# Splitting every attention step of heads 3 to 32, with a product moved to GpSimd and TensorE's order left to the scheduler

## The chip, the cores and the metric

The kernel runs on one core of a Trainium2 chip. The metric is device time in microseconds (us) of one execution, from launch to end. Five engines work side by side, each through its own queue in order: TensorE (PE; PEld is its weight load), VectorE (DVE), ScalarE (ACT), GpSimd (POOL) and SyncE (SP), which issues the DMAs. An instruction that waits for a semaphore holds up everything behind it on its engine.

## The reference

Three layers in a row, all in float32:

```
# 1: attention with pooled queries, B=4, H=8 (32 heads), S=1152, D=64, T=576 pooled queries
q_pool = q.reshape(B, H, S // 2, 2, D).mean(axis=3)
scores = scale * q_pool @ k.T;  attn = softmax(scores);  x = attn @ v
# 2: four experts of causal attention over T=576, each token weighted by the top 2 of a gate
logits = x @ w_gate
for e in range(4): out += weight_e * (softmax(causal(q_e k_e.T)) @ v_e @ wo[e])
# 3: channel mixing, with the token before mixed in (mu)
k = relu(xk @ w_k);  v = k * k @ w_v;  out = sigmoid(xr @ w_r) * v
```

## The kernel before

Layer 1 goes through 32 heads (index 0 to 31; the title counts from 1). A head is nine steps. Step `si` of `s1_job` takes two tiles of 128 keys against 288 queries each: `qk` (L778, L779) multiplies into a PSUM tile `st` (two of them rotate), `ew` takes the exponential on ScalarE (L786) into `p`, and `pv` multiplies `p` by the values, four steps later (`LAG`), into an accumulator `bank` (four PSUM banks rotate among all users).

High precision comes from splitting: a float32 number is written as a rounded high part (fp32r) and the rest, and products of the parts are summed. For `pv` there are two forms, chosen for each step by the tables `S0` and `S1`. A step marked `'sv'` is split: ScalarE copies `p` to its high part `ph` (L64), VectorE subtracts to get `pl` (L71), and `pv` is three fp32r matmuls (L813, L814, L815). A step marked `'n'` is not split: `pv` is one float32 matmul (L806), which the profile shows as two records. Before, steps 0, 3 and 6 of every head from the third on are `'n'`.

Beside these steps run tasks, put at places between steps by tables of start and end: the load of a later head's q, k and v; its preparation `s1_prep` (transposes, splits into `sk`, then `dup_q` and `dup_k`, 14 DMAs per head that copy the parts to `QA`, `QB`, `KA`, `KB` and the small block `BD`); and `s1_max`, which finds each query's largest score (L735 and L750 on TensorE, L737 and L751 on VectorE). Its end, `max_finish`, transposes the maxima (L402), copies them to `mr` (L403, VectorE) and sends them by DMA to a row of `QB` (L410, L411). `L779` of the next head reads that row, so a head can't complete its first step before the row has landed. `normaliser` fetches each head's row sums by DMA (`sd`), inverts them, and brings them back spread over partitions (`R`); L835 multiplies by it into `XT`, on VectorE. From the ninth head on, the work of layer 2 for the batch before stands between the steps, and the splitting of layer 3's weights (`w3st`) runs on VectorE and ScalarE.

Order: a scheduler orders each engine's instructions by its own estimate of when they can start, except that from three steps ahead of head 2 to the end of the heads TensorE keeps the order in which the program is written (L1095, `manual_schedule`).

Of the kernel before, what the change touches and what calls it, by code (L numbers as in the profile page):

```python
# [55 lines left out]
def tile_kernel(ctx: ExitStack, tc: tile.TileContext, q, k, v, w_gate, wq, wk, wv, wo,  # L56
                mu_k, mu_r, w_k, w_v, w_r, out):
    nc = tc.nc
    LAG, LO, HB = G["LAG"], G["LO"], G["HB"]
# [14 lines left out]
    T = S // 2  # L74
# [9 lines left out]
    HT = T // 2  # L84
# [39 lines left out]
    def f32(ap):  # L124
        return ap.bitcast(F32)
# [12 lines left out]
    def act_hi(dst, src):  # L138
        nc.scalar.activation(dst, src, AF.Copy)
# [14 lines left out]
    def later(n, fn):  # L154
        pending.append((now[0] + n, fn))
# [13 lines left out]
    def drive(steps, tasks, drain=False, first=0):  # L169
        def fill(t):  # L170
            for x in tasks:
                x.run(t)

        for i, st in enumerate(steps, first):
            now[0] += 1
            if st.qk:
                st.qk()
            if st.ew:
                st.ew()
            lagged.append(st)  # L180
            if len(lagged) > LO and lagged[-1 - LO].ew2:
                lagged[-1 - LO].ew2()
                lagged[-1 - LO].ew2 = None
            pv = lagged.pop(0).pv if len(lagged) > LAG else ()
            m = len(pv) + 1
            for j in range(m):
                fill(i + (j + 1) / m - 1e-6)
                if j < len(pv):
                    pv[j]()
            run_later()  # L190
        if drain:
            for st in lagged:
# [353 lines left out]
    def s2_out(b):  # L546
        def make(dt):
# [12 lines left out]
            def ew():  # L560
# [36 lines left out]
    BD = [s1.tile([P, P], F32R, name=f"BD{i}") for i in range(2)]  # L597
# [29 lines left out]
    def s1_prep(hh):  # L627
        first = hh < G["nf1"]
        kr, qr = raw.pop(hh)
        i = hh % NK  # L630
        own = (slice(0, D), slice(D, P))
        KAi, KBi, QAi, QBi = KA[i], KB[i], QA[i], QB[i]
        qp = s1a.tile([QW, NQ * D], F32, tag="qp", name=f"qp{hh}")
        sk = None if first else s1a.tile([P, 2, SW + HT], F32R, tag="sk", name=f"sk{hh}")
# [44 lines left out]
        qhalf = (slice(0, HT), slice(HT, T))  # L679
# [201 lines left out]
    CW = G["CW"]  # L881
# [68 lines left out]
    steps, tasks = [], []  # L950
# [61 lines left out]
    for hh in range(NH):  # L1012
        z = "0" if hh < H else "1"
        if hh + 1 < NH:
# [311 lines left out]
```

## Time and profile before

| | us |
|---|---|
| median of 3 runs (lowest, highest) | 1110.75 (1109.9, 1113.37) |
| the profiled execution's own time | 1113.59 |
| its span, first to last instruction | 1111.9 |
| TensorE busy, share of the span | 1030.4, 93% |
| VectorE busy, share | 788.0, 71% |
| ScalarE busy, share | 582.7, 52% |
| GpSimd busy, share | 183.5, 17% |
| mean granted TensorE clock | 0.970 |

The shares are averages over unlike stages: the heads take about the first 760 us, the last batch's layer 2 and layer 3 the rest, in which VectorE and ScalarE do much less. TensorE's records overlap (a matmul's record starts while the one before still drains), so its busy time is more than its work; the distance from one start to the next tells what a matmul costs.

### The profile page before, as it was taken

What the parts mean: (1) busy time and instruction counts of PE and PEld (TensorE: products, weight loads), DVE (VectorE), ACT (ScalarE), POOL (GpSimd) and SP (SyncE); (2) the same over time, 40 slices, a digit from 0 to 9 for tenths busy, and PEclk for the clock granted to TensorE, in tenths of its full rate; (3) what the DMA queues carried; (4) which work ended last, traced back from release to release, by engine and by line L of the source; (5) the groups of instructions that cost most, each with busy time, mean ns of one, the idle gap of its engine ahead of it and who ended that gap; (6) DMA issues with size and microseconds to landing.
All of it is one profiled execution on the core that took longest, in us unless ns stands there. A gap on an engine that the chain in (4) does not pass through costs nothing.

```text
span 1111.9 us, 18276 instructions
## 1 busy us (share of the span) xinstructions
PE 1030.4 (93%) x6450; PEld 892.8 (80%) x6450; DVE 788.0 (71%) x1647; ACT 582.7 (52%) x999; POOL 183.5 (17%) x279
## 2 busy tenths in 40 slices
PE   6898999999988899998989999989898799999998
PEld 4687888987777797787779888878776688888887
DVE  5787887888779679888878777786867534444442
ACT  5456777566556456666656566664455212222222
POOL 6223111110212000120110011021012001111110
PEclk9899999999999999999999999999998899999999
DMA  4556666646544664565456544337345321111100
GB/s 112 140 130 150 132 152 146 158 117 156 133 121 104 156 156 123 146 163 136 108 122 180 126 114 108 86 100 221 122 138 163 110 81 39 38 38 39 39 19 19
DMA packets 144397, 129.08 MB, mean 116 GB/s; under 512 B 71401, under 2 KB 106658, under 8 KB 144306
## 3 DMA queue, kind: packets, MB, share of 16 engines
q1 hardware_dynamic: 144306, 127.92, 44.9%
q8 instruction: 51, 0.84, 0.3%
q14 instruction: 40, 0.33, 0.1%
HBM read 63.24 MB, written 20.07 MB: 75 GB/s over the span
## 4 chain that ended last, share of the span: by engine, by line
PE 56%; DVE 16%; DMA 15%; SPq 4%; ACT 4%; issue 3%; POOL 2%; DVEq 0%; ACTq 0%; POOLq 0%
PE stw L1159 9%; PE sth L1123 7%; PE str L1146 4%; PE bank L806 4%; PE stq L348 4%; PE st L778 3%; PE st L779 3%; PE bank L735 3%; DVE PM L737 3%; DMA R<-scr 3%; DVE pl L71 3%; PE bank L504 3%; PE bank L813 2%; PE bank L814 2%; PE stv L281 2%
## 5 line engine op out<-in xcount | busy, mean ns | idle before, releaser
L786 ACT ACTIVATE p<-st 128x576 f32<-128x576 f32 x288 | 186.1, 647 | 130.6 <-PE st L779 123.5
L737 DVE TENSOR_REDUCE PM<-bank 128x1 f32<-128x384 f32 (+1 forms) x390 | 208.3, 547 | 48.7 <-PE bank L735 46.5
L778 PE MATMUL st<-QA,KA 128*128 128x288 f32 x576 | 186.1, 336 | 2.5 <-ACT p L786 2.0
L779 PE MATMUL st<-QB,KB 65*128 65x288 f32 x576 | 167.3, 304 | 0.3 <-DMA QB<-mr 0.3
L735 PE MATMUL bank<-KA,QA 128*128 128x384 f32 (+1 forms) x390 | 154.8, 408 | 11.7 <-DVE KB L145 3.6
L71 DVE TENSOR_TENSOR pl<-p,ph 128x576 fp32r<-128x576 f32 x190 | 147.1, 775 | 21.8 <-ACT ph L64 19.9
L64 ACT ACTIVATE ph<-p 128x576 fp32r<-128x576 f32 x190 | 129.6, 683 | 19.3 <-PE bank L814 12.6
L778 PEld LDWEIGHTS st<-QA,KA 128*128 128x128 f32 x576 | 113.2, 197 | 14.0 <-ACT p L786 3.2
L806 PE MATMUL bank<-p,VF 128*65 128x288 f32 x384 | 118.6, 406 | 0.2
L779 PEld LDWEIGHTS st<-QB,KB 65*128 65x128 f32 x576 | 113.5, 197 | 3.9 <-DMA QB<-mr 0.7
L813 PE MATMUL bank<-ph,VV 128*65 128x288 f32 x384 | 115.4, 300 | 1.3 <-DVE sk L145 1.0
L815 PE MATMUL bank<-pl,VV 128*65 128x288 f32 x384 | 114.2, 298 | 0.0
L814 PE MATMUL bank<-ph,VV 128*64 128x288 f32 x384 | 114.1, 297 | 0.0
L735 PEld LDWEIGHTS bank<-KA,QA 128*128 128x128 f32 (+1 forms) x390 | 77.2, 200 | 28.8 <-DVE PM L737 5.3
L71 POOL TENSOR_TENSOR VV<-VF,VV 128x576 fp32r<-128x576 f32 x32 | 43.0, 1345 | 307.7 <-ACT VV L64 292.3
L1123 PE MATMUL sth<-xkh,wk 128*128 128x256 f32 x512 | 91.4, 279 | 1.2 <-ACT relu L1130 1.2
L1130 ACT ACTIVATE relu<-sth 128x512 f32<-128x512 f32 x32 | 17.5, 596 | 122.9 <-PE sth L1123 122.1
L1123 PEld LDWEIGHTS sth<-xkh,wk 128*128 128x128 f32 x512 | 78.7, 188 | 1.8 <-ACT relu L1130 1.4
L1123 PE MATMUL sth<-xkl,wk 128*128 128x256 f32 x256 | 71.4, 279 | 0.0
L504 PE MATMUL bank<-p,V 128*65 128x288 f32 (+5 forms) x288 | 63.1, 351 | 6.0 <-DVE PM L737 4.6
L806 PEld LDWEIGHTS bank<-p,VF 128*65 128x65 f32 x384 | 51.4, 137 | 15.2 <-DVE PM L417 0.9
L490 POOL TENSOR_SCALAR_AFFINE_SELECT p<-p 128x128 f32<-128x128 f32 (+1 forms) x96 | 32.6, 370 | 176.0 <-ACT p L482 172.1
(212 smaller groups left out, 2262.6 us busy)
## 6 DMA issues: line engine op xcount, KB each, us to landing
KA<-sk SPq DMA_DIRECT2D x60, 160.0 KB
qr<-in_q_dram SPq DMA_DIRECT2D x32, 288.0 KB
kr<-in_k_dram SPq DMA_DIRECT2D x32, 288.0 KB
VF<-in_v_dram SPq DMA_DIRECT2D x32, 288.0 KB
QA<-sk SPq DMA_DIRECT2D x120, 72.0 KB
KA<-sk SPq DMA_DIRECT2D x60, 128.0 KB
R<-scr SPq DMA_DIRECT2D x48, 144.0 KB
w3h<-w3st SPq DMA_DIRECT2D x20, 256.0 KB
```

What stands on the lines that cost most here:

```text
L64: nc.scalar.activation(dst, src, AF.Copy)
L71: eng[e].tensor_tensor(dst, src, hi.bitcast(F32), op=ALU.subtract)
L735: nc.tensor.matmul(ps[:n, : 3 * P], QA[i][:, t0 : t0 + n], KA[i][:, 3 * g * P : 3 * (g + 1) * P], start=True, stop=True)
L737: nc.vector.tensor_reduce(pm[:n, c, g : g + 1], ps[:n, : 3 * P], axis=AX.X, op=ALU.max)
L778: nc.tensor.matmul(st[:, n, :HT], KA[i][:, ks], QA[i][:, cs], start=True, stop=False)
L779: nc.tensor.matmul(st[:, n, :HT], KB[i][0 : D + 1, ks], QB[i][0 : D + 1, cs], start=False, stop=True)
L786: nc.scalar.activation(pt, st[:, :, :HT], AF.Exp, scale=1.0 / 16.0)
L806: nc.tensor.matmul(a[: D + 1, :HT], VF[hh % NF][:, c], cell["p"][:, n], start=c == 0, stop=c == NC - 1)
L813: nc.tensor.matmul(a[: D + 1, :HT], vh, ph[:, n], start=c == 0, stop=False)
L814: nc.tensor.matmul(a[:D, :HT], vl, ph[:, n], start=False, stop=False)
L815: nc.tensor.matmul(a[: D + 1, :HT], vh, pl[:, n], start=False, stop=c == NC - 1)
L1123: nc.tensor.matmul(st[:, f // 2, f % 2 * GT : (f % 2 + 1) * GT], w[kt][:, fs], x[:, kt], start=i == 0, stop=i == 3 * KT - 1)
```

## The change

In the table of constants, the keys that change (an entry's place is a step's number where it is a list; positions are in steps relative to a head's first):

| key | before | after | what it sets |
|---|---|---|---|
| `S0`, `S1` | `'n'` at 0, 3, 6, else `'sv'` | `'sv'` at all nine | form of `pv`, heads 3 to 32 |
| `HB` | 3 | 4 | buffers of `ph` and of `pl` |
| `PB` | 6 | 5 | buffers of `p` |
| `xt`, `xt0` | `'v'` | `'g'` | engine of the normalising product: VectorE, GpSimd |
| `mx0`, `mx1` | (-4.5, 4.5) | (-4.2, 4.0) | start and end of `s1_max` |
| `nm` | 1 | 2 | steps from the maxima to their transpose |
| `dup` | 2 | 1 | steps from the split of `sk` to its DMAs |

The rest of the diff:

```diff
@@ max_finish
             nc.tensor.transpose(ps[:5, :P], f32(nm), ident)
-            nc.vector.tensor_copy(mr, ps[:5, :P])
+            act_hi(mr, ps[:5, :P])
@@ s1_prep
-            later(G["dup"], dup_q)
-            later(G["dup"], dup_k)
+            later(G["dup"], dup)
...
-        def dup_q():
+        def dup():
+            n = T % P
+            for up in range(2):
+                nc.sync.dma_start(f32(BD[hh % 2][own[up], up * D : up * D + n]), f32(sk[own[1], 0, SW + HT - n :]))
             for up in range(2):
                 a, z, cs = own[up], own[1 - up], qhalf[up]
                 nc.sync.dma_start(f32(QAi[a, cs]), f32(sk[a, 0, SW:]))
                 nc.sync.dma_start(f32(QAi[z, cs]), f32(sk[a, 1, SW:]))
-                nc.sync.dma_start(f32(QBi[0:D, cs]), f32(sk[a, 0, SW:]))
-            n = T % P
+            dup_k()
             for up in range(2):
-                nc.sync.dma_start(f32(BD[hh % 2][own[up], up * D : up * D + n]), f32(sk[own[1], 0, SW + HT - n :]))
+                nc.sync.dma_start(f32(QBi[0:D, qhalf[up]]), f32(sk[own[up], 0, SW:]))
@@ the end of the heads
-    with tc.manual_schedule(engines={mybir.EngineType.PE}):
-        drive(steps[free:], tasks, drain=True, first=free)
+    drive(steps[free:], tasks, drain=True, first=free)
```

Lines after L709 move by one (L778 becomes L779, and so on). What the order looks like at three places follows; in names, `st1_5_0` is step 0 of head index 5, `ph1_4_6` the high part of step 6 of head index 4, and the last number only counts tiles.

TensorE at an unsplit step, before: step 6 of head index 4, between steps 1 and 2 of the next head.

```order
L778 MATMUL st1_5_1_1593<-QA2_173,KA2_171 128x288
L779 MATMUL st1_5_1_1593<-QB2_174,KB2_172 128x288
L806 MATMUL bank139_1557<-p1_4_6_1498,VF0_185 65x288
L735 MATMUL bank144_1605<-KA0_175,QA0_177 128x384
L806 MATMUL bank139_1557<-p1_4_6_1498,VF0_185 65x288
L778 MATMUL st1_5_2_1627<-QA2_173,KA2_171 128x288
L779 MATMUL st1_5_2_1627<-QB2_174,KB2_172 128x288
```

The same step after, where the head's first steps are also completed.

```order
L736 MATMUL bank143_1659<-KA0_175,QA0_177 128x384
L814 MATMUL bank140_1626<-ph1_4_6_1558,VV0_183 65x288
L815 MATMUL bank140_1626<-ph1_4_6_1558,VV0_183 64x288
L816 MATMUL bank140_1626<-pl1_4_6_1559,VV0_183 65x288
L780 MATMUL st1_5_0_1637<-QB2_174,KB2_172 128x288
L779 MATMUL st1_5_0_1637<-QA2_173,KA2_171 128x288
L780 MATMUL st1_5_0_1637<-QB2_174,KB2_172 128x288
L780 MATMUL st1_5_1_1676<-QB2_174,KB2_172 128x288
L779 MATMUL st1_5_1_1676<-QA2_173,KA2_171 128x288
L780 MATMUL st1_5_1_1676<-QB2_174,KB2_172 128x288
L736 MATMUL bank144_1687<-KA0_175,QA0_177 128x384
```

Each float32 matmul has become three, and steps 0 and 1 of the head now complete together, after half of step 6 of the head before.

TensorE at a head's start, before: the last transposes for a later head, then step 0 of head index 5 in one piece, ahead of step 5 of head index 4.

```order
L699 MATMUL bank141_1564<-ident_112,kr7_1375 128x128
L685 MATMUL bank141_1564<-ident_112,qp7_1504 128x96 x3
L778 MATMUL st1_5_0_1571<-QA2_173,KA2_171 128x288
L779 MATMUL st1_5_0_1571<-QB2_174,KB2_172 128x288
L778 MATMUL st1_5_0_1571<-QA2_173,KA2_171 128x288
L779 MATMUL st1_5_0_1571<-QB2_174,KB2_172 128x288
L735 MATMUL bank142_1579<-KA0_175,QA0_177 128x384
L813 MATMUL bank139_1557<-ph1_4_5_1477,VV0_183 65x288
```

After: only the parts of steps 0 and 1 that do not read the row of maxima are begun there.

```order
L779 MATMUL st1_5_0_1637<-QA2_173,KA2_171 128x288
L779 MATMUL st1_5_1_1676<-QA2_173,KA2_171 128x288
L649 MATMUL bank137_1594<-ident_112,kr7_1436 128x128 x4
L736 MATMUL bank138_1615<-KA0_175,QA0_177 128x384
L736 MATMUL bank139_1623<-KA0_175,QA0_177 128x384
L814 MATMUL bank140_1626<-ph1_4_4_1502,VV0_183 65x288
L815 MATMUL bank140_1626<-ph1_4_4_1502,VV0_183 64x288
L816 MATMUL bank140_1626<-pl1_4_4_1503,VV0_183 65x288
```

Between this and the completion shown above stand half of step 4, all of step 5 and half of step 6 of the head before, four blocks of `s1_max` and the transposes for a later head.

GpSimd before, in the early heads: sums of query pairs (`qp`) and the low part of the values (`VV`), between splits of weights.

```order
L639 TENSOR_TENSOR qp6_1271<-qr6_1141 96x384
L142 TENSOR_SCALAR wo_h_141<-wst103_1112 128x512
L148 TENSOR_TENSOR wo_l_142<-wst103_1112,wo_h_141 128x512
L891 COPY w3st0_2456<-XT_154 1x1
L71 TENSOR_TENSOR VV0_183<-VF0_185,VV0_183 128x9x64
```

GpSimd after, at heads 6 to 8: one product into `XT` per head.

```order
L639 TENSOR_TENSOR qp7_1562<-qr7_1437 96x384
L71 TENSOR_TENSOR VV1_184<-VF1_186,VV1_184 128x9x64
L836 TENSOR_TENSOR XT_154<-U1_3_1364,R1_3_1492 64x2x3x96
L639 TENSOR_TENSOR qp8_1819<-qr8_1694 96x384
L71 TENSOR_TENSOR VV0_183<-VF0_185,VV0_183 128x9x64
```

GpSimd now does a third two-input operation per head, which was VectorE's.

## Rows read from the trace of the kernel before

**Rows 1.** Busy time by stretch (start:end, length, busy us and records of each engine).
```profile
85.20:191.40 106.20, 99.99 (x644) 87.03 (x643) 83.67 (x162) 73.94 (x124) 20.18 (x18) 0.98 0.64 144
191.40:370.60 179.20, 166.08 (x1077) 142.95 (x1075) 148.97 (x328) 111.61 (x197) 25.67 (x40) 0.97 0.55 134
sum 662.00, PE 620.83 PEld 539.60 DVE 534.23 ACT 416.09 POOL 97.55; mean PE 155.21 PEld 134.90 DVE 133.56 ACT 104.02 POOL 24.39
400.00:500.00 100.00, 94.98 (x649) 83.62 (x648) 85.10 (x193) 62.80 (x113) 14.02 (x21) 1.00 0.58 147
```
**Rows 2.** The same for five single heads (order: PE, PEld, DVE, ACT, POOL, clock).
```profile
123.40:140.30 16.90, 16.69 (x108) 14.22 (x107) 14.06 (x29) 12.41 (x21) 2.33 (x2) 1.00 0.67 145
175.40:191.40 16.00, 16.00 (x110) 14.39 (x109) 12.07 (x25) 12.00 (x20) 2.13 (x2) 1.00 0.64 147
219.00:243.30 24.30, 22.99 (x148) 18.84 (x147) 23.34 (x54) 14.93 (x27) 4.35 (x9) 1.00 0.51 131
292.90:327.70 34.80, 28.55 (x169) 23.57 (x168) 25.50 (x59) 19.09 (x34) 4.52 (x8) 0.92 0.54 133
327.70:353.30 25.60, 22.85 (x145) 18.77 (x144) 23.62 (x54) 16.20 (x29) 4.08 (x9) 0.98 0.41 102
```
**Rows 3.** TensorE's timeline (start us, length, line): split products, then unsplit.
```profile
400.59 0.29 PE L813 MATMUL bank<-ph,VV 128*65 128x288 f32 x1
400.73 0.29 PE L814 MATMUL bank<-ph,VV 128*64 128x288 f32 x1
400.85 0.30 PE L815 MATMUL bank<-pl,VV 128*65 128x288 f32 x1
400.99 0.34 PE L735 MATMUL bank<-KA,QA 128*128 128x384 f32 x1
401.17 0.29 PE L778 MATMUL st<-QA,KA 128*128 128x288 f32 x1
...
403.90 0.65 PE L806 MATMUL bank<-p,VF 128*65 128x288 f32 x2
404.18 0.55 PE L735 MATMUL bank<-KA,QA 128*128 128x384 f32 x1
404.57 0.40 PE L806 MATMUL bank<-p,VF 128*65 128x288 f32 x1
```
**Rows 4.** Groups by line (count, then busy us, mean ns, then idle before, releaser).
```profile
L71 DVE TENSOR_TENSOR pl<-p,ph 128x576 fp32r<-128x576 f32 x190 | 147.1, 775 | 21.8 <-ACT ph L64 19.9 <-issue 0.2
L64 ACT ACTIVATE ph<-p 128x576 fp32r<-128x576 f32 x190 | 129.6, 683 | 19.3 <-PE bank L814 12.6 <-DVE pl L71 1.3 <-DVE PM L737 0.7
L71 POOL TENSOR_TENSOR VV<-VF,VV 128x576 fp32r<-128x576 f32 x32 | 43.0, 1345 | 307.7 <-ACT VV L64 292.3 <-PE bank L685 11.9 <-PE st L779 3.5
L639 POOL TENSOR_TENSOR qp<-qr 96x384 f32<-96x384 f32 x31 | 33.1, 1067 | 147.2 <-PE bank L685 86.1 <-DMA qr<-in_q_dram 41.8 <-PE bank L735 7.4
L835 DVE TENSOR_TENSOR XT<-U,R 64x576 f32<-64x576 f32 x32 | 25.0, 782 | 14.7 <-DMA R<-scr 14.3
L403 DVE CAST mr<-bank 5x128 fp32r<-5x128 f32 x43 | 11.6, 270 | 0.1
```
**Rows 5.** One low part on VectorE beside GpSimd: GpSimd's timeline, then VectorE's.
```profile
190.26 1.33 POOL L71 TENSOR_TENSOR VV<-VF,VV 128x576 fp32r<-128x576 f32 x1 [11.90 <-PE bank L685]
...
190.79 1.42 DVE L71 TENSOR_TENSOR pl<-p,ph 128x576 fp32r<-128x576 f32 x1 [0.90 <-ACT ph L64]
```
**Rows 6.** The tile `pl`: shortest, median, longest ns.
```profile
L71 DVE TENSOR_TENSOR pl<-p,ph x190: 686/748/1422, 38.2 to 761.4; 128x576 fp32r<-128x576 f32 x190
```
**Rows 7.** TensorE's waits from 85 to 760 us (total us, times, longest).
```profile
PE bank L750 <- DMA BD<-sk: 5.0, 4, 3.2
PE bank L504 <- DVE PM L737: 4.6, 2, 2.6
PE bank L699 <- DVE sk L145: 4.5, 5, 1.8
PE sto L556 <- ACT YH L64: 4.5, 2, 2.5
```
**Rows 8.** SyncE's issues, after the transpose of maxima (last row, TensorE) of head 5.
```profile
116.86 0.66 SPq L410 DMA_DIRECT2D QB<-mr  x1
119.11 0.50 SPq L251 DMA_DIRECT2D scr<-rd  x1
119.66 0.59 SPq L411 DMA_DIRECT2D QB<-ml  x1
...
114.34 0.27 PE L402 MATMUL bank<-ident,nm 128*5 128x128 f32 x1
```

More of the change, by code (lines that the diff above doesn't have):

```diff
@@ L25 @@
 D = 64
-G = {'LAG': 4, 'LO': 2, 'nf1': 2, 'nfx': 1, 'mxA': (0, 5), 'mxB': (-1.0, 5.5), 'mxC': (-3.5, 5.0), 'prA': (0.5, 5.0), 'prB': (-1.5, 2.0), 'mx0': (-4.5, 4.5), 'mx1': (-4.5, 4.5), 'vl': (0.0, 1.5), 'vs': (5.5, 1.0), 'pr0': (-3.0, 1.0), 'pr1': (-3.0, 1.0), 'ldA': (5.5, 5.0), 'ldB': (2.5, 2.0), 'ld': (1.5, 1.0), 'm2': (2.0, 3.0), 'nm': 1, 'nm2': 1, 'dup': 2, 'mid': 1, 'bc': 1, 'end': 9, 'mid2': 2, 'end2': 4, 'spl': 9, 'gate': 8, 'gate2': 2, 'w2': (2, 30), 'w3': (7, 14), 'S0': ('n', 'sv', 'sv', 'n', 'sv', 'sv', 'n', 'sv', 'sv'), 'S1': ('n', 'sv', 'sv', 'n', 'sv', 'sv', 'n', 'sv', 'sv'), 've': 'g', 'kh0': 's', 'kh1': 's', 'qh0': 's', 'qh1': 's', 'kq': 's', 'kl': 'v', 'rs': 'v', 'rl': 'v', 'ym': 'g', 'yo': 'v', 'LGe': 'v', 'p1': (5, 5, 5, 9), 'p2': (9, 9, 9), 'p3': (2,), 'p4': (9, 9, 9, 9), 'p5': (8, 8, 8, 8), 'p6': (9, 9, 9), 'po': (2, 4, 5, 9), 'add0': 'g', 'add1': 'g', 'xt': 'v', 'u1': 's', 'u2': 's', 'y2': 'v', 'yh': 's', 'yl': 'v', 'xo': 'v', 'v2': 's', 'xh': 's', 'xl': 'v', 'vvh': 's', 'vvl': 'g', 'klo': 'v', 'HB': 3, 'PB': 6, 'blk': 1, 'm2w': 2, 'order': 2, 'kdup': 0, 'L2': 4, 'O2': 1, 'a0': (5.0, 5.0), 'a1': (2.0, 2.5), 'a2': (0.0, 1.0), 'a3': (2.0, 2.0), 'r0': 2, 'NV': 2, 'NF': 2, 'SA': ('n', 'vg', 'sg', 'n', 'sv', 'n', 'sv', 'sv', 'sv'), 'SB': ('n', 'sv', 'sv', 'n', 'vv', 'n', 'sv', 'sv', 'sv'), 'ua': 'v', 'u0': 's', 'xt0': 'v', 'w3d': 8, 'w3q': (3, 27), 'WC': 1, 'kb': 1, 'kst': 1, 'qst': 0, 'CW': 512, 'wt': 'v', 'wl': 'v', 'wa': 'v', 'WB': 1, 'mxg': 4, 'hq': 's', 'hpos': (0, 1, 11, 20)}
@@ new lines @@
+G = {'LAG': 4, 'LO': 2, 'nf1': 2, 'nfx': 1, 'mxA': (0, 5), 'mxB': (-1.0, 5.5), 'mxC': (-3.5, 5.0), 'prA': (0.5, 5.0), 'prB': (-1.5, 2.0), 'mx0': (-4.2, 4.0), 'mx1': (-4.2, 4.0), 'vl': (0.0, 1.5), 'vs': (5.5, 1.0), 'pr0': (-3.0, 1.0), 'pr1': (-3.0, 1.0), 'ldA': (5.5, 5.0), 'ldB': (2.5, 2.0), 'ld': (1.5, 1.0), 'm2': (2.0, 3.0), 'nm': 2, 'nm2': 1, 'dup': 1, 'mid': 1, 'bc': 1, 'end': 9, 'mid2': 2, 'end2': 4, 'spl': 9, 'gate': 8, 'gate2': 2, 'w2': (2, 30), 'w3': (7, 14), 'S0': ('sv', 'sv', 'sv', 'sv', 'sv', 'sv', 'sv', 'sv', 'sv'), 'S1': ('sv', 'sv', 'sv', 'sv', 'sv', 'sv', 'sv', 'sv', 'sv'), 've': 'g', 'kh0': 's', 'kh1': 's', 'qh0': 's', 'qh1': 's', 'kq': 's', 'kl': 'v', 'rs': 'v', 'rl': 'v', 'ym': 'g', 'yo': 'v', 'LGe': 'v', 'p1': (5, 5, 5, 9), 'p2': (9, 9, 9), 'p3': (2,), 'p4': (9, 9, 9, 9), 'p5': (8, 8, 8, 8), 'p6': (9, 9, 9), 'po': (2, 4, 5, 9), 'add0': 'g', 'add1': 'g', 'xt': 'g', 'u1': 's', 'u2': 's', 'y2': 'v', 'yh': 's', 'yl': 'v', 'xo': 'v', 'v2': 's', 'xh': 's', 'xl': 'v', 'vvh': 's', 'vvl': 'g', 'klo': 'v', 'HB': 4, 'PB': 5, 'blk': 1, 'm2w': 2, 'order': 2, 'kdup': 0, 'L2': 4, 'O2': 1, 'a0': (5.0, 5.0), 'a1': (2.0, 2.5), 'a2': (0.0, 1.0), 'a3': (2.0, 2.0), 'r0': 2, 'NV': 2, 'NF': 2, 'SA': ('n', 'vg', 'sg', 'n', 'sv', 'n', 'sv', 'sv', 'sv'), 'SB': ('n', 'sv', 'sv', 'n', 'vv', 'n', 'sv', 'sv', 'sv'), 'ua': 'v', 'u0': 's', 'xt0': 'g', 'w3d': 8, 'w3q': (3, 27), 'WC': 1, 'kb': 1, 'kst': 1, 'qst': 0, 'CW': 512, 'wt': 'v', 'wl': 'v', 'wa': 'v', 'WB': 1, 'mxg': 4, 'hq': 's', 'hpos': (0, 1, 11, 20)}
```

## The prediction

> **What bounds the kernel now.** I read the busy times by stretch first, then single heads, then the line groups, the waits and the timeline. From 85.2 to 747.2 us, which holds 28 heads, TensorE shows 620.8 us of 662 busy, VectorE 534.2 and ScalarE 416.1 [rows 1]. That is 94%, 81% and 63%, so TensorE leads, but it is not alone. By head there are three kinds. In sixteen of the 28 TensorE is idle for 1.2 us or less and VectorE for 2.8 us or more; two of them stand in the rows, of 16.9 and 16.0 us [rows 2]. In three it is VectorE that hardly rests: the head at 219.0 us has it busy for 23.34 of 24.3 us, the one at 327.7 for 23.62 of 25.6 [rows 2], and the one that starts at 426.5 is the third. The other nine leave both engines time; the head at 292.9 takes 34.8 us with TensorE at 28.55 and VectorE at 25.50 [rows 2]. There what counts is who waits for whom, not work. The last stage, after the heads, is left as it is but for one product ahead of it.
>
> **The change part by part.** *Splitting the unsplit steps, TensorE.* Three fp32r products take 0.40 us from the first one's start to the next instruction (400.59 to 400.99) [rows 3]. A float32 product and the block of L735 between take 0.67 us (403.90 to 404.57), and such a block alone 0.18 (400.99 to 401.17), so the product costs 0.49 us. The change saves 0.09 us on each: 6 per head are 0.54 us, 180 in 30 heads are 16.2 us. This is all the work that TensorE is spared.
>
> *The same, on the other engines.* Each of the 90 steps gets a high part, 0.683 us on ScalarE, and a low part, 0.775 us on VectorE [rows 4]: 61.5 and 69.8 us. Moving L835 to GpSimd takes 32 times 0.782 us, 25.0 us, off VectorE, and moving `mr` to ScalarE 11.6 us [rows 4]. VectorE's net is +33 us before contention, ScalarE's about +73.
>
> *The product on GpSimd.* No row shows it there. GpSimd's two-input operation of 576 elements takes 1.345 us, that of 384 elements 1.067 us [rows 4]; I take 1.35, so 43 us more on an engine that is busy for 97.6 of 662 us [rows 1]. Its own time is hidden, since `XT` is read by the next batch's splits only; in the last head it is on the way to the last stage and costs 1.35 - 0.78 = 0.6 us. What it does to VectorE is not hidden. One low part began 0.53 us after a GpSimd operation of 1.33 us and took 1.42 us [rows 5], where the median is 0.748 [rows 6]: 0.67 us lost. Bounds: below, nothing, if the operations miss each other; above, 32 times 0.67, 21 us. In between, the 190 low parts have a mean of 0.775 and a median of 0.748, which is 5.1 us lost beside 76 us of GpSimd's work [rows 4, 6]; with 43 us more of that work and 280 low parts it would be 5.1 x 119/76 x 280/190 = 11.8, so +7 us. I take 7.
>
> The Trainium skill (SBUF — State Buffer, Who interferes with whom) says that a VectorE operation with two SBUF inputs and a GpSimd operation that reads SBUF exclude each other, the later one waiting for the whole of the first. The row of 1.42 us agrees: it ends 0.62 us after GpSimd's. By that rule every low part that meets an `XT` product from behind is held, and the upper bound of 21 us would be the price; the mean over all rows says that the queues seldom meet so badly.
>
> VectorE's total is thus +40 us, some 1.4 us per head, and its share of the stretch rises from 0.807 to (534.2 + 39)/662 = 0.866. No long stretch has that: the best 100 us show 0.851, the best batch 148.97/179.2 = 0.831 [rows 1]. ScalarE goes to 485 us, 0.73.
>
> *Buffers.* With four `ph` and `pl` and a lag of four steps, the high part of step i waits for the product of step i-4, which stands right behind step i's scores. ScalarE waited 12.6 us for L814 in all before [rows 4]. I expect the same, since three buffers for two of three steps last hardly longer. Bounds: 0, and one set of three products, 0.40 us, on each of 270 high parts, 108 us, against 662 - 416 - 73 = 173 us that ScalarE would still idle. `p` is free after the low part now, so five are enough.
>
> *The row of maxima and the DMAs.* The transpose of the maxima moves half a step later, some 0.9 us. In the head shown SyncE issued its two DMAs 2.5 and 5.3 us after the transpose [rows 8], and the next head's first exponential came 9.1 us after it (123.4) [rows 2, 8]. The margin was small. After the change the scheduler finishes steps 0 and 1 later and together, as the order shows. I count this as nothing, because TensorE has other products in between; what it costs if ScalarE lacks work is a rival below. Each head still issues 14 DMAs for `dup`, but earlier and with `BD` first: this should take away most of the 5.0 us that L750 waited for it [rows 7].
>
> *TensorE's order.* Apart from head starts the new order is nearly the written one. Its use is with waits that hold up unlike work: the four largest come to 18.6 us (5.0 + 4.6 + 4.5 + 4.5) [rows 7]. Behind most of them VectorE is late, and stays late, so I take a third, 6.2 us. Bounds: all 18.6 back, or as much lost, if the scheduler's estimate of times is off.
>
> *Sum.* In sixteen heads the 0.54 us count: -8.6. In three VectorE's 1.4 us count: +4.2. In nine neither. Order and `BD`: -6.2. Together -10.6 on the profiled execution's 1113.6 (span 1111.9): 1103.0. That execution lay 2.8 us above the median of the runs, so the forecast is 1100.
>
> **The rivals.** *VectorE becomes the bound.* It would need 573 us in the stretch. If no long run of heads gets it past the 0.851 of its best 100 us, the stretch takes 573/0.851 = 674 us, 12 more than now, and the median 1123; at the best batch's 0.831 it takes 690 and 1139. It decides from a share of 0.866. For it: the heads at 219.0 and 327.7 us run at 0.96 and 0.92. Against: these also show that VectorE can be kept that busy, with TensorE at 22.99 of 24.3 us in the first.
>
> *A hole on ScalarE at each head's start.* From the last scores of one head to the completed step 0 of the next there now stand fifteen products, four blocks of `s1_max` and the transposes; before it was six products, one such block and fewer transposes. Nine products and three blocks at 0.13 and 0.18 us are 1.7 us more without scores. ScalarE idles for 4.5 and 4.0 us in the plain heads [rows 2]; it gets 2.3 us more work per head (3 x 0.683 + 0.27). If its idle time can't fall under the 4.0, such a head takes 12.0 + 2.3 + 4.0 = 18.3 us instead of 16 to 17: 1.5 us in nine plain heads, +13.5, and with about 4 us saved elsewhere 1120. Against it: the lag of four steps leaves TensorE products to do meanwhile.
>
> *The scheduler's order pays in full.* If it recovers all 18.6 us of waits and the 16.2 us of work count everywhere, the median is 1110.75 - 34.8 = 1076. Against: nine heads wait for chains that no order shortens.
>
> *Nothing moves.* The saved 0.54 us per head become waits for VectorE, which is at 0.83 in the middle batches already, and the new order, so close to the old, does nothing: 1111.
>
> **How the numbers follow.** Chances: forecast 0.38, order in full 0.12, nothing 0.14, VectorE as bound 0.24, hole on ScalarE 0.12. About 0.3%, 3.3 us, is what a measurement of this kernel can tell from no change. So faster 0.50, same 0.14, slower 0.36. The forecast's own range is 1090 to 1107. For eight in ten I go from 1078, just above the order in full, to 1130, between VectorE's two prices.
>
> **What would show it.** Right: no float32 `pv` products from the third head on, TensorE's records as close as before, the sixteen heads about 0.5 us shorter, VectorE's share in the heads near 0.87, and few waits of TensorE for `BD`. VectorE as bound: its idle time nearly gone and TensorE waiting for `PM` and `pl`. Hole: ScalarE idle for some 4 us before a head's first exponential, with TensorE idle soon after. The contention shows in low parts of 1.4 us beside `XT`, and in their mean, which I expect near 0.79 us. I am wrong if the heads together take as long or longer, or if the gain lies in heads where TensorE was not the bound.

## The result and the profile after

The median of four runs is 1078.81 us (1074.21 to 1085.47) against 1110.33 (1105.85 to 1113.37) for the kernel before: a ratio of 0.9726, interval [0.9681, 0.977]. The same kernel in a later series gave 0.9732 [0.9698, 0.9766]. The forecast of 1100 had the direction, but a third of the gain. The profiled execution took 1079.04 us (span 1077.3), 0.2 above its median; the profiled one of before lay 2.8 above its own, so of the 34.6 us between the two traces some 32 are the change.

Names: heads count from 0, as in [rows 8], where head 5 starts at 123.4 us. A head starts with its first exponential. Heads 3 to 30 are the 28 heads of the prediction, heads 3 to 8 have no work of layer 2 beside them. In the attention's code behind `dup` a line of after, and of the runs made from it, stands one number higher than in before (L735 is L736, L835 is L836).

First the busy time by stretch of after, which answers [rows 1] (start:end, length, busy us and records of TensorE, its weight loads, VectorE, ScalarE, GpSimd, then the granted clock, DMA share, GB/s): heads 3 to 8, heads 9 to 30, and the sum over both.

```profile
87.10:191.40 104.30, 96.97 (x679) 90.60 (x679) 92.69 (x170) 83.46 (x148) 30.71 (x24) 0.98 0.62 146
191.40:712.10 520.70, 497.91 (x3526) 457.43 (x3525) 472.29 (x998) 381.96 (x696) 117.70 (x138) 1.00 0.56 138
sum 625.00, PE 594.88 PEld 548.02 DVE 564.99 ACT 465.42 POOL 148.41; mean PE 297.44 PEld 274.01 DVE 282.49 ACT 232.71 POOL 74.20
```

The 28 heads take 625.0 us instead of 662.0. Heads 9 to 30 of before are one row more:

```profile
191.40:747.20 555.80, 520.84 (x3416) 452.56 (x3414) 450.55 (x995) 342.15 (x598) 77.37 (x120) 0.98 0.53 131
```

So 35.1 of the 37.0 us lie in heads 9 to 30 and 1.9 in heads 3 to 8. Ahead of head 3 after is 1.9 us later, and the last stage takes the same (352.6 and 352.5 us after the last exponential). VectorE now stands at 564.99/625 = 0.904 and in heads 9 to 30 at 472.29/520.70 = 0.907.

The same for single heads of after, which answer [rows 2]: heads 5, 8, 10, 13, 14, 21.

```profile
123.70:140.50 16.80, 15.90 (x116) 14.88 (x115) 15.59 (x30) 14.14 (x25) 4.12 (x4) 1.00 0.62 145
174.50:191.40 16.90, 15.58 (x113) 14.74 (x113) 14.38 (x27) 13.44 (x25) 4.40 (x4) 1.00 0.64 149
217.70:240.60 22.90, 21.93 (x159) 20.11 (x158) 22.01 (x52) 17.37 (x32) 5.63 (x9) 1.00 0.58 143
286.30:314.40 28.10, 24.59 (x173) 22.11 (x172) 21.89 (x50) 19.59 (x36) 4.83 (x8) 1.00 0.48 123
314.40:340.10 25.70, 23.67 (x158) 21.03 (x157) 23.97 (x52) 18.61 (x35) 6.40 (x10) 0.96 0.49 115
479.30:504.70 25.40, 24.41 (x172) 21.89 (x170) 24.41 (x54) 20.12 (x38) 7.41 (x8) 1.00 0.56 146
```

Heads 5 and 14 last as long as before, head 8 0.9 us longer. Head 13 went from 34.8 to 28.1 us [rows 2], head 21 from 30.0 to 25.4. Summed over the prediction's three kinds of heads (starts by the first exponential; TensorE's idle time is length less busy time):

| heads | before | after | change | predicted | TensorE idle before, after |
|---|---|---|---|---|---|
| sixteen, TensorE leads | 351.9 | 339.8 | -12.1 | -8.6 | 7.5, 11.5 |
| three, VectorE busy | 75.3 | 72.0 | -3.3 | +4.2 | 6.0, 4.5 |
| nine with time left (3, 11, 13, 16, 19, 21, 22, 24, 30) | 234.8 | 213.2 | -21.6 | 0 | 27.7, 14.1 |

The groups by line of after, which answer [rows 4] (count, busy us, mean ns, then idle before and its releasers):

```profile
L71 DVE TENSOR_TENSOR pl<-p,ph 128x576 fp32r<-128x576 f32 x280 | 229.7, 824 | 10.2 <-ACT ph L64 9.5
L836 POOL TENSOR_TENSOR XT<-U,R 64x576 f32<-64x576 f32 x32 | 49.2, 1539 | 159.2 <-DMA R<-scr 127.0 <-DVE PM L738 22.5 <-PE bank L816 9.3
L64 ACT ACTIVATE ph<-p 128x576 fp32r<-128x576 f32 x280 | 189.6, 684 | 20.1 <-PE bank L815 11.4 <-ACT p L787 0.9 <-ACT U L134 0.6
L139 ACT ACTIVATE mr<-bank 5x128 fp32r<-5x128 f32 x43 | 10.9, 254 | 5.3 <-PE bank L402 5.3
```

The product on GpSimd takes 1539 ns, and a low part 824 ns where it took 775. TensorE's waits of after from 85 to 760 us, which answer [rows 7] (total us, times, longest):

```profile
PE bank L649 <- DMA kr<-in_k_dram: 5.6, 6, 1.8
PE st L779 <- ACT p L787: 4.1, 10, 1.1
PE bank L736 <- ACT U L134: 3.6, 2, 2.0
PE bank L504 <- DVE PM L738: 3.3, 2, 2.5
```

The wait for `BD`, the largest before, is in no row of this view any more, nor is that of `sto` for `YH`. Those for `kr` and `p` have come up in their place.

### The profile page after: what moved, and what is told of

The parts are those of the page before. It is cut to its first block, busy times and chain, and to the rows that moved or that the text cites. A ratio compares the mean times of both kernels' runs of the same rounds, so it can differ in the third digit from the quotient of the medians.

```text
span 1077.3 us, 19012 instructions
## 1 busy us (share of the span) xinstructions
PE 1007.3 (94%) x6630; PEld 906.5 (84%) x6630; DVE 820.9 (76%) x1662; ACT 635.7 (59%) x1132; POOL 241.9 (22%) x311
## 5 line engine op out<-in xcount | busy, mean ns | idle before, releaser
L71 DVE TENSOR_TENSOR pl<-p,ph 128x576 fp32r<-128x576 f32 x280 | 229.7, 824 | 10.2 <-ACT ph L64 9.5
L64 ACT ACTIVATE ph<-p 128x576 fp32r<-128x576 f32 x280 | 189.6, 684 | 20.1 <-PE bank L815 11.4
L779 PE MATMUL st<-QA,KA 128*128 128x288 f32 x576 | 175.6, 316 | 5.7 <-ACT p L787 4.3
L814 PE MATMUL bank<-ph,VV 128*65 128x288 f32 x564 | 168.4, 299 | 2.0 <-ACT ph L64 1.3
L816 PE MATMUL bank<-pl,VV 128*65 128x288 f32 x564 | 166.9, 296 | 0.3 <-DVE pl L71 0.3
L815 PE MATMUL bank<-ph,VV 128*64 128x288 f32 x564 | 166.5, 295 | 0.0
L736 PE MATMUL bank<-KA,QA 128*128 128x384 f32 (+1 forms) x390 | 143.9, 383 | 12.6 <-DVE KB L145 4.4
L779 PEld LDWEIGHTS st<-QA,KA 128*128 128x128 f32 x576 | 111.6, 194 | 16.3 <-ACT p L787 9.8
L736 PEld LDWEIGHTS bank<-KA,QA 128*128 128x128 f32 (+1 forms) x390 | 76.0, 199 | 23.8 <-ACT U L134 4.8
L836 POOL TENSOR_TENSOR XT<-U,R 64x576 f32<-64x576 f32 x32 | 49.2, 1539 | 159.2 <-DMA R<-scr 127.0
L814 PEld LDWEIGHTS bank<-ph,VV 128*65 128x65 f32 x564 | 77.4, 137 | 5.8 <-ACT ph L64 1.6
L815 PEld LDWEIGHTS bank<-ph,VV 128*64 128x64 f32 x564 | 76.5, 136 | 6.0
L816 PEld LDWEIGHTS bank<-pl,VV 128*65 128x65 f32 x564 | 76.7, 136 | 1.9 <-DVE pl L71 0.9
```

The source lines that it names most:

```text
L71: eng[e].tensor_tensor(dst, src, hi.bitcast(F32), op=ALU.subtract)
L736: nc.tensor.matmul(ps[:n, : 3 * P], QA[i][:, t0 : t0 + n], KA[i][:, 3 * g * P : 3 * (g + 1) * P], start=True, stop=True)
L779: nc.tensor.matmul(st[:, n, :HT], KA[i][:, ks], QA[i][:, cs], start=True, stop=False)
L814: nc.tensor.matmul(a[: D + 1, :HT], vh, ph[:, n], start=c == 0, stop=False)
L815: nc.tensor.matmul(a[:D, :HT], vl, ph[:, n], start=False, stop=False)
L816: nc.tensor.matmul(a[: D + 1, :HT], vh, pl[:, n], start=False, stop=c == NC - 1)
```

## The experiments

Each run was timed beside the kernel before, and a ratio is to before in the same series: e1 to e4, e5 to e8 and, on another chip, e9 to e12 (medians of before 1108.04, 1106.02 and 1106.23 us).

Sums by heads and stretches come from one profiled execution of each kernel. That of before, 1113.59 us, lies 5 to 8 us above these medians, so differences between traces come out larger than those between medians. The changed kernel was profiled twice (after and e10): its three kinds of heads took 339.8 and 341.1, 72.0 and 72.1, 213.2 and 212.8 us.

My theory after the result: the change of TensorE's order is the gain, and the rest of the edit moves little. The rival: splitting, with the shift of work to ScalarE and GpSimd, is the gain. The first four runs do each alone and undo each alone.

**e1_before_sched: the scheduler's order alone, on the kernel before.**

```diff
-    with tc.manual_schedule(engines={mybir.EngineType.PE}):
-        drive(steps[free:], tasks, drain=True, first=free)
+    drive(steps[free:], tasks, drain=True, first=free)
```

> The kernel before with one edit: TensorE's order is the scheduler's in all heads. Theory 1 (the order did it: heads in which TensorE stood behind unlike waits got shorter): 1085 to 1095 us against 1110, with the heads at index 13, 21 and 22 some 4 to 6 us shorter. Theory 2 (the splitting did it): within 4 us of 1110. Theory 3 (the earlier DMAs with BD first and the new positions did it): within 4 us of 1110, and the 5 us that TensorE waits for BD stay.

Measured: 1080.17 us, 0.9738 [0.9709, 0.9766], below theory 1's range. Heads 13, 21 and 22 are 9.0, 3.5 and 3.0 us shorter, where 4 to 6 had been expected. Two lines, with no work saved, give 28 us; the whole change gave 31.5 and 28.4 in its two series.

**e2_after_written: the changed kernel with the written order put back** (the same lines the other way round).

> The changed kernel with one edit: TensorE keeps the written order from three steps ahead of head index 1 on, as before. Theory 1: back up to 1100 or more of the 1110. Theory 2 and theory 3: within 5 us of 1079.

Measured: 1100.15 us, 0.9935 [0.9905, 0.9964]. All the rest of the change gives 8 us. The two stretches of e1, heads 3 to 8 and heads 9 to 30 (columns as in the stretches of after):

```profile
86.90:196.50 109.60, 102.57 (x637) 87.92 (x636) 85.31 (x163) 73.89 (x124) 21.88 (x17) 0.97 0.59 138
196.50:711.90 515.40, 501.26 (x3389) 441.95 (x3388) 441.98 (x988) 340.69 (x596) 79.75 (x114) 1.00 0.56 138
```

and those of e2:

```profile
88.20:188.50 100.30, 94.37 (x683) 90.23 (x682) 89.36 (x170) 83.98 (x148) 24.98 (x20) 0.99 0.62 147
188.50:732.80 544.30, 510.72 (x3549) 462.54 (x3547) 479.55 (x1003) 386.30 (x698) 122.11 (x143) 0.98 0.54 133
```

Between these traces the order alone takes 40.4 us off heads 9 to 30 (555.8 to 515.4) and adds 3.4 to heads 3 to 8 (106.2 to 109.6). The rest alone takes 5.9 off heads 3 to 8 and 11.5 off heads 9 to 30. So where heads are plain the written order is the better one, and the scheduler's pays where the work of layer 2 stands between the steps.

How it pays can be seen at one place. This is TensorE's timeline of before in head 16 (start us, length, line, operation; in brackets the idle time ahead of it and what ended it), where layer 2's out product needs `YH`:

```profile
372.70 0.29 PE L556 MATMUL sto<-YH,wo_h 128*128 128x288 f32 x1
372.83 0.30 PE L556 MATMUL sto<-YL,wo_h 128*128 128x288 f32 x1
372.96 0.29 PE L556 MATMUL sto<-YH,wo_l 128*128 128x288 f32 x1
375.74 0.40 PE L556 MATMUL sto<-YH,wo_h 128*128 128x288 f32 x1 [2.48 <-ACT YH L64]
```

VectorE's and ScalarE's rows of before that lead to this `YH`, with what each waited for:

```profile
374.22 0.75 DVE L537 TENSOR_TENSOR U<-U,R 64x576 f32<-64x576 f32 x1 [0.77 <-DMA R<-scr]
...
375.01 0.68 ACT L64 ACTIVATE YH<-U 64x576 fp32r<-64x576 f32 x1 [1.89 <-DVE U L537]
```

`R` comes back late from DRAM; VectorE and ScalarE themselves stand idle, 0.77 and 1.89 us. TensorE has products of the running head to do, but they stand behind the fourth `sto` product in its queue, which it works off in order. In e1, at the same place of head 16, TensorE's timeline reads:

```profile
364.06 0.29 PE L556 MATMUL sto<-YH,wo_l 128*128 128x288 f32 x1
364.19 0.29 PE L813 MATMUL bank<-ph,VV 128*65 128x288 f32 x1
...
364.98 0.34 PE L735 MATMUL bank<-KA,QA 128*128 128x384 f32 x1
365.16 0.29 PE L778 MATMUL st<-QA,KA 128*128 128x288 f32 x1
...
365.82 0.29 PE L814 MATMUL bank<-ph,VV 128*64 128x288 f32 x1
367.33 0.40 PE L556 MATMUL sto<-YH,wo_h 128*128 128x288 f32 x1 [1.22 <-ACT YH L64]
```

and ScalarE's row for the same `YH`:

```profile
366.60 0.68 ACT L64 ACTIVATE YH<-U 64x576 fp32r<-64x576 f32 x1 [2.38 <-DVE U L537]
```

The chain is no shorter: ScalarE waits even longer, 2.38 us. But thirteen products of the attention, the scores of a step among them (L778 and L779), have moved in between. The wait halves, from 2.48 to 1.22 us.

In head 13 it is VectorE that TensorE waits for (L504, the second of [rows 7]), but VectorE stands behind a DMA in its own queue, that of a weight for layer 3. TensorE's row of before, then VectorE's:

```profile
323.06 1.06 PE L504 MATMUL bank<-p,V 128*65 128x128 f32 x8 [2.03 <-DVE PM L737]
...
322.02 0.43 DVE L906 TENSOR_SCALAR w3st<-w3st 128x512 int32<-128x512 int32 x1 [2.75 <-DMA w3st<-in_moe_w_k_dram]
322.37 0.55 DVE L737 TENSOR_REDUCE PM<-bank 128x1 f32<-128x384 f32 x1
```

TensorE has six waits of more than 1.5 us in heads 9 to 30 of before, of 1.8 to 2.6 us, 13.0 in all. Four end so in a DMA (twice `R`, once `w3st`, once `KA`); in the other two, up to 263.8 and 525.7 us, VectorE was busy throughout. In e1 and e5 no wait of TensorE there is over 1.5 us.

After these waits TensorE's clock fell. Further on in head 16 of before, TensorE's timeline and a stretch read:

```profile
377.25 0.44 PE L556 MATMUL sto<-YH,wo_h 128*128 128x288 f32 x1
377.49 0.44 PE L556 MATMUL sto<-YL,wo_h 128*128 128x288 f32 x1
...
376.50:379.90 3.40, 3.29 (x14) 3.21 (x15) 0.81 (x2) 0.00 (x0) 0.00 (x0) 0.50 0.63 137
```

The granted clock is 0.50, the lower of its two levels (1.2 GHz), and the products start 0.24 us apart, where they were 0.13 apart ahead of the wait (372.70 to 372.96). Within 2.3 us of the end of each of the six waits the granted clock fell so, for 23.9 us in all in heads 9 to 30 of before; in e2 it is 20.5 us, in after 3.4, in e5 3.4 (there without so long a wait before it) and in e1 none.

Over heads 9 to 30 TensorE is idle for 35.0 us in before, 14.1 in e1, 22.8 in after and 33.6 in e2; gaps of more than 0.3 us make up 28.9, 11.9, 20.2 and 28.5 of it.

**e3_before_split: splitting all steps alone, on the kernel before.**

```diff
-... 'S0': ('n', 'sv', 'sv', 'n', 'sv', 'sv', 'n', 'sv', 'sv'), ... 'HB': 3, 'PB': 6, ...
+... 'S0': ('sv', 'sv', 'sv', 'sv', 'sv', 'sv', 'sv', 'sv', 'sv'), ... 'HB': 4, 'PB': 5, ...
```

(`S1` as `S0`.)

> The kernel before with the steps of heads 3 to 32 all split (four buffers of ph and pl, five of p); order, engines and positions as before. Theory 2: 1085 to 1095 us. Theory 1: VectorE gets 70 us and gives nothing away, so 1105 to 1125. Theory 3: 1105 to 1125 as well.

Measured: 1103.24 us, 0.994 [0.9912, 0.9968], 5 us less than before, which is outside the ranges of all three theories. Its heads 9 to 30:

```profile
191.30:741.30 550.00, 511.69 (x3554) 465.70 (x3552) 490.07 (x1061) 382.25 (x665) 82.71 (x120) 0.98 0.54 133
```

TensorE is busy for 511.69 us, where it was 520.84 in before, but idle for 38.3, where it was 35.0, and the stretch is 5.8 us shorter. By kinds of heads, the sixteen where TensorE led got longer, 354.9 us against 351.9, with TensorE idle for 17.9 instead of 7.5; the three went from 75.3 to 74.0 and the nine from 234.8 to 226.5.

**e4_after_unsplit: the changed kernel with steps 0, 3 and 6 unsplit again** (the edit of e3 the other way round).

> The changed kernel with steps 0, 3 and 6 of heads 3 to 32 unsplit again (three buffers of ph and pl, six of p). Theory 2: 1095 or more. Theory 1: TensorE's 16 us of work come back, of which half counts: 1083 to 1090. Theory 3: within 5 us of 1079.

Measured: 1091.27 us, 0.9843 [0.9816, 0.9871], 12 us above the changed kernel, between the ranges of theories 1 and 2. In the traces it lies in the sixteen heads (353.0 us against 339.8). So both count: the order gives 28 us by itself, the splitting 5 by itself and 12 on top. The rival as the whole cause falls. But e4, which has the order too, is also 11 us slower than e1: where the splitting is missing, the other parts of the change (positions, DMAs, `XT`, `mr`) cost time.

To separate the order's two effects, the next runs switch between written and scheduled order at head 9, where layer 2 comes in.

**e5_before_mix: the kernel before, written order up to head 9, the scheduler's from there.**

```diff
-    with tc.manual_schedule(engines={mybir.EngineType.PE}):
-        drive(steps[free:], tasks, drain=True, first=free)
+    moe = at_[9][0] - 3
+    with tc.manual_schedule(engines={mybir.EngineType.PE}):
+        drive(steps[free:moe], tasks, first=free)
+    drive(steps[moe:], tasks, drain=True, first=moe)
```

> The kernel before with the written order kept only to three steps ahead of head index 9 (the plain heads) and the scheduler's order from there on, where layer 2's work stands between the steps. Theory A (the order pays where unlike work meets and costs some 3 us in the plain heads, as heads 3 to 8 took 106.2 us before and 109.6 with the scheduler's order): 1073 to 1080, at or below the 1080 with the scheduler's order in all heads. Rival (any change of order has its luck, the gain is not tied to the place): between 1085 and 1108.

Measured: 1077.16 us, 0.9735 [0.9706, 0.9763], within theory A's range.

**e9_before_rev: the other way round, the scheduler's order up to head 9, written from there.**

> The kernel before with the scheduler's order in the plain heads (to three steps ahead of head index 9) and the written order from there on: the complement of the run that had it the other way round. Theory A (the order pays only where layer 2's work stands between the steps): 1105 to 1115, no gain. Rival (the two halves share the 28 us): 1090 to 1100.

Measured: 1111.56 us, 1.0044 [1.0025, 1.0064], within theory A's range: 0.4% slower than before. The two stretches of e5:

```profile
83.80:188.10 104.30, 99.47 (x644) 86.81 (x643) 83.62 (x162) 74.17 (x124) 20.20 (x18) 0.98 0.64 145
188.10:707.70 519.60, 505.00 (x3400) 444.87 (x3399) 442.60 (x991) 341.55 (x597) 79.11 (x115) 1.00 0.55 137
```

and TensorE's waits of e9 from 188 to 760 us, the first and the third row of which are those of [rows 7] again:

```profile
PE sto L556 <- ACT YH L64: 4.9, 2, 2.6
...
PE bank L504 <- DVE PM L737: 3.6, 2, 2.7
```

The gain of the order is all in heads 9 to 30. In e5, where nothing but the order differs, the sixteen heads got 6.3 us shorter, the three 4.1, and the nine 27.7, of which 17.7 were idle time of TensorE (27.7 to 10.0). In the nine (head 3 is one of them) the time at the clock's lower level went from 24.9 to 6.8 us.

**e6_after_mix: the changed kernel with the same switch at head 9.**

> The changed kernel with the written order in the plain heads (index 1 to 8) and the scheduler's from index 9 on. Theory A: 1074 to 1077, some 3 us below the changed kernel, with heads 3 to 8 at about 100 us as with the written order throughout, against 104.3. Rival: 1079 to 1090.

Measured: 1073.09 us, 0.9694 [0.9669, 0.9718]; 0.4% under the changed kernel's ratio of the later series, the intervals just overlap. It is just under theory A's range. Its heads 3 to 8 took 100.3 us, as in e2, against 104.3.

**e7_before_split_sched: e1 and e3 together.**

> The kernel before with two edits, the scheduler's order and all steps split; XT and mr stay on VectorE, positions and DMAs as before. Theory A (order is all, splitting is a wash because VectorE gets what TensorE is spared): 1076 to 1086. Rival (splitting pays 16 us of TensorE's work once the order no longer holds it up): 1064 to 1072.

Measured: 1073.62 us, 0.972 [0.969, 0.9751], between the two ranges. With the order of e1 the splitting is worth 0.2% more, which the intervals don't separate, where e4 had shown it at 12 us. What the splitting is worth thus depends on what else is in, between 2 and 12 us, and I can't say on what.

```profile
187.40:702.20 514.80, 498.05 (x3519) 454.81 (x3518) 479.48 (x1054) 377.63 (x662) 88.97 (x112) 1.00 0.57 139
```

In these heads 9 to 30 VectorE is busy for 479.48/514.80 = 0.931 of the time. So a share of 0.9 does not make it the bound.

**e8_after_xt_vector: the changed kernel with the normalising product back on VectorE.**

```diff
-... 'xt': 'g', ... 'xt0': 'g', ...
+... 'xt': 'v', ... 'xt0': 'v', ...
```

> The changed kernel with the normalising product back on VectorE. If the contention with GpSimd eats what VectorE is spared (low parts at a mean of 824 ns against 748 undisturbed, 21 us in all, against 25 us of products): within 4 us of 1079, and the mean of the low parts back at about 780 ns. If VectorE is the bound and the move relieves it: 1085 to 1095.

Measured: 1072.08 us, 0.9689 [0.9661, 0.9717], below both ranges; the mean of the low parts came out as expected in the first. Its groups (columns as in the groups of after):

```profile
L71 DVE TENSOR_TENSOR pl<-p,ph 128x576 fp32r<-128x576 f32 x280 | 217.8, 782 | 3.6 <-ACT ph L64 2.8
L836 DVE TENSOR_TENSOR XT<-U,R 64x576 f32<-64x576 f32 x32 | 26.4, 824 | 3.0 <-DMA R<-scr 2.5
```

The product takes 26.4 us on VectorE. On GpSimd it makes a low part 42 ns longer on average (824 to 782), 280 x 0.042 = 11.8 us on VectorE. The means of e10 and e12, 825 and 786 ns, repeat this.

**e10_after_again: the changed kernel unaltered, for the comparisons within this series.**

> The changed kernel unaltered, so that the other three of this round can be read against it on one chip: 1076 to 1081.

Measured: 1077.79 us, 0.9732 [0.9698, 0.9766].

**e11_after_old_dma: the changed kernel with the maxima's positions and the order of the DMAs of before** (`mx0`, `mx1`, `nm`, `dup` and the two functions `dup_q` and `dup_k` as they were).

```diff
-... 'mx0': (-4.2, 4.0), 'mx1': (-4.2, 4.0), ... 'nm': 2, ... 'dup': 1, ...
+... 'mx0': (-4.5, 4.5), 'mx1': (-4.5, 4.5), ... 'nm': 1, ... 'dup': 2, ...
-            later(G["dup"], dup)
+            later(G["dup"], dup_q)
+            later(G["dup"], dup_k)
...
```

> The changed kernel with the positions of s1_max (-4.5, 4.5), nm 1, dup 2, and the two functions dup_q and dup_k as before (BD after QA and QB). If the earlier DMAs and the new positions carry part of the gain: 1085 or more, and TensorE waits for BD again. If the order alone carries it: within 4 us of the changed kernel.

Measured: 1083.55 us, 0.9792 [0.9761, 0.9824]: 0.6% slower than e10, with intervals that barely touch, and between the two expectations. The positions and the DMAs' order are worth some 6 us. TensorE's wait for `BD` is back at 0.8 us from 85 to 760 us (3.1 in the whole execution), so it does not make up the 6 us; the sixteen heads take 351.4 us, where e10's take 341.1.

**e12_after_mix_xt_vector: e6 and e8 together**, the version that the runs pointed to.

> The changed kernel with the normalising product back on VectorE and the written order in the plain heads (index 1 to 8): the two edits that were each some 6 us faster in single runs. If they add up: 1064 to 1070. If both only move the same waits: 1070 to 1075.

Measured: 1069.02 us, 0.9653 [0.9624, 0.9683], the fastest of all: 8.8 us under the changed kernel (e10) and 37.2 under the kernel before, both in the same series, and within the range for edits that add up. Its heads 9 to 30:

```profile
190.20:704.90 514.70, 498.86 (x3528) 458.05 (x3527) 475.37 (x1020) 381.42 (x696) 85.83 (x114) 1.00 0.56 140
```

The product on GpSimd thus shows in two pairs, e10 against e8 (0.9732, 0.9689) and e6 against e12 (0.9694, 0.9653): 0.4% slower both times. In each pair the intervals overlap; the mean of the two, with their spreads taken as independent, is 0.42% ± 0.29%. Each pair has one run from each of the last two series, the second pair the other way round, so that a difference between the series cancels in the mean. The product on GpSimd costs some 4.6 us and is no part of the gain.

## Why the prediction was right or wrong

**The step that failed is that on TensorE's order.** The prediction said: "Behind most of them VectorE is late, and stays late, so I take a third, 6.2 us", from four waits of 18.6 us, and of the nine heads "In nine neither". Alone the order gives 28 us (e1), and in e5 27.7 of the profiled 38 us come from those nine heads. So the term of 6.2 us for order and `BD` measured 28 for the order alone. It is also what the prediction had named as a sign of being wrong: the gain lies in heads where TensorE was not the bound. Four things were wrong in the step.

- What is late was taken from the engine named in [rows 7]. In head 16 the chain behind `YH` began with a DMA, and VectorE and ScalarE were idle with it; in head 13 the VectorE that was waited for was itself waiting for a DMA. So it is with four of the six long waits in heads 9 to 30; behind the other two VectorE was busy, as the prediction had it. That "nine heads wait for chains that no order shortens" fits the chain of head 16, which is no shorter in e1 (ScalarE waits for 2.38 us), but it does not matter: the order needs only to put independent products ahead of the waiting one.
- The four largest rows, 18.6 us, were taken for the whole. TensorE's idle time in the 28 heads is 662.0 - 620.8 = 41.2 us [rows 1], and that of the nine heads, 27.7 us, could have been read from the same view as [rows 2].
- A wait was counted with its own length only. The products behind it ran at the lower clock: in the nine heads 24.9 us of before and 6.8 of e5 were at that level. By the distances of 0.24 and 0.13 us this is, as an estimate, 18.1 x (1 - 0.13/0.24) = 8.3 us, which with the 17.7 us of idle time makes 26.0 of the 27.7.
- "Apart from head starts the new order is nearly the written one" is what the order at plain heads shows; in heads 9 to 30, where thirteen products moved past one, it doesn't hold.

"The scheduler's order pays in full", the rival at 1076, is the nearest, 3 us off, and that is luck, for its sum is wrong: it added 18.6 us of waits to 16.2 of spared work. The order alone paid 28 (e1); all the rest paid 8 without it (e2) and 0 to 4 on top of it (28.4 and 31.5 for the whole change).

**TensorE's spared work.** The term of -8.6 in sixteen heads came out at -12.1, and that it is near is luck in part: the order alone makes -6.3 (e5), and the splitting alone +3.1 (e3). In e3 TensorE's busy time there fell by 7.3 us, so the work was spared, but its idle time rose by 10.4. Alone, the splitting gained in the nine heads (-8.3), where it had been put at nothing. On top of the order it gained 0.5 us in the sixteen, 3.0 in the three and 4.6 in the nine (e1 to e7); with the other parts of the change present it gained 13.2 in the sixteen (e4 to after).

**VectorE.** The share was put at 0.866; it is 0.904, part of that because the stretch got shorter. The three heads, in which VectorE's added work was to cost 4.2 us, took 3.3 less, and 1.3 less with the splitting alone (e3). (The third of them, at 426.5 us, did not fit its kind: VectorE was idle for 3.1 us in it and TensorE for 2.0.) VectorE as the bound, the rival at 1123 to 1139, is refuted by after, e7 and e12 with 0.907, 0.931 and 0.924 over 515 to 521 us. The best 100 us of a trace were no limit of the engine: even with the written order e3 shows 490.07/550.00 = 0.891 over a whole stretch.

**The product on GpSimd.** It was put at 1.35 us and takes 1.54. The loss in low parts was put at 11.8 us in all (a mean of 0.79); it is (824 - 748) x 280 = 21 us, with after's tile `pl` beside it, which answers [rows 6] (shortest, median, longest ns):

```profile
L71 DVE TENSOR_TENSOR pl<-p,ph x280: 685/746/1912, 39.2 to 729.0; 128x576 fp32r<-128x576 f32 x140
```

The median is unmoved and the longest went from 1422 to 1912 ns. That one, in after's timelines of GpSimd and VectorE, answers [rows 5]:

```profile
592.25 1.42 POOL L836 TENSOR_TENSOR XT<-U,R 64x576 f32<-64x576 f32 x1 [13.68 <-DMA R<-scr]
...
592.38 1.91 DVE L71 TENSOR_TENSOR pl<-p,ph 128x576 fp32r<-128x576 f32 x1
```

The low part began 0.13 us after GpSimd's product and ended 0.62 us after its end (594.29 and 593.67), as the one in [rows 5] did. This agrees with what the Trainium skill (SBUF — State Buffer, Who interferes with whom) says, that the later of two such operations waits for the whole of the first. In e2 a low part met two GpSimd operations in a row:

```profile
558.96 1.42 POOL L836 TENSOR_TENSOR XT<-U,R 64x576 f32<-64x576 f32 x1 [10.82 <-DMA R<-scr]
560.34 1.01 POOL L639 TENSOR_TENSOR qp<-qr 96x384 f32<-96x384 f32 x1
...
559.27 2.70 DVE L71 TENSOR_TENSOR pl<-p,ph 128x576 fp32r<-128x576 f32 x1
```

It ended 0.62 us after the second (561.97 and 561.35). Over the whole of after, 73 of the 280 low parts overlap a GpSimd operation and take 1.05 us on average; the other 207 take 0.745. How often they meet isn't set by GpSimd's work alone: with the product on VectorE the mean is 782 ns in e8 and 810 in e3.

**The hole on ScalarE at a head's start** (1120) did not come. In plain heads its idle time is 16.80 - 14.14 = 2.7 us in head 5 and 3.5 in head 8, under the 4.0 below which it was not to fall. A smaller cost of the order is there all the same: heads 3 to 8 take 104.3 us in after with ScalarE idle for 20.8, and 100.3 with the written order (e2) with ScalarE idle for 16.3.

**The row of maxima and the DMAs.** That the wait for `BD` goes was right. It was counted within the 6.2. The positions and the DMAs' order are worth some 6 us by e11, of which TensorE's wait for `BD` itself is 0.8 us from 85 to 760 us; what the rest is was not shown.

**Whether the clock is the gain.** It is a part. Two executions of before with a mean granted clock of 0.979 took 1102.22 and 1103.70 us, two of e1 with the same 1081.53 and 1081.69: 21 of the 28 us remain at an equal clock.

**What stays open.** Of the 40.4 us by which e1's heads 9 to 30 are shorter, 20.9 are idle time of TensorE (35.0 to 14.1) and, by the estimate above, 23.9 x (1 - 0.13/0.24) = 11.0 the clock; the rest is not explained. Nor is why the splitting is worth 12 us in one surrounding and 2 in another.

## What to carry to other kernels

Before the gain of another order is sized, each wait is to be followed to the end of its chain: if the chain ends in a DMA while all engines idle, anything independent that stands behind the waiting instruction in an in-order queue can fill the hole. The gain is then nearer to the idle time of the heads concerned than to a share of the largest waits, and what the lower clock costs after a wait comes on top. An order written out by hand can be the better one where the work is regular and the worse one where a second chain is woven in; both can be used in one kernel, each where it wins (e6, e12). An operation moved to GpSimd to relieve VectorE is to be charged with what it does to VectorE's own operations: here 11.8 of the 25 us spared, and 0.4% more time.

## What had not been expected of the hardware

VectorE ran at 0.907 to 0.931 of the time for over 500 us, with TensorE at 0.96 to 0.97 beside it (after, e7, e12). A low part met by one GpSimd operation took up to 1.91 us in after, 2.6 times its median of 0.746, and one met by two in a row 2.70 us in e2. In before, TensorE's six longest waits in heads 9 to 30 cost more than their 13.0 us: the granted clock fell to 0.50 within 2.3 us of the end of each, for 23.9 us in all.
